# A new order of steps in a fused FFT and mixture kernel: fewer warming products, the first pair's maxima ahead of the next pair's folds, the third pair's product inside the last pair's

## The chip, the cores and the metric

The kernel runs on one core of one Trainium2 chip. The metric is device time in microseconds (us), the median of the runs of one kernel. The engines are PE (TensorE), DVE (VectorE), ACT (ScalarE), POOL (GpSimd) and SP, which issues every DMA of this kernel. Each engine works through its own queue in order.

## The reference, cut to what matters

```python
X = np.fft.fft(x, axis=1)            # x: 8 x 2496 x 256
X = np.fft.fft(X, axis=2).real       # then rows of 256: N = 19968 tokens
logits = x @ phi                     # 32 slots
d = exp(logits - logits.max(0)); d /= d.sum(0) + 1e-9     # over tokens
slot_input = d.T @ x                 # 8 experts x 4 slots
h = np.maximum(slot_input[e] @ w1[e], 0.0); slot_out[e] = h @ w2[e]
c = exp(logits - logits.max(1)); c /= c.sum(1) + 1e-9     # over slots
out = c @ slot_out                   # 19968 x 256
```

All data are float32. The input is 20 MB, the weights w1 and w2 are 17 MB, the output is 20 MB.

## The kernel before, in words

The eight sequences are handled as four pairs, p = 0 to 3. The Fourier transform is split (2496 = 39 x 64) and is never written out: its first steps give the logits, and the product of the softmax with the tokens is taken back to x through the transform. Each pair goes through the same chain of steps. A step has a letter, then the pair, then a part (t, half, or block), so `u20` is the product u of pair 2, first half. What each does, with its line and engine:

- f and F (L275, POOL, some DVE): fold a tile of x with its mirror tile xm, both loaded by SP (L208, L209); the mirror tiles share five buffers. F and A are second halves of tiles that are worked in halves.
- a and A (L304, DVE): transposes; z (L319, PE): first transform stage; t (L339, DVE): transposes out of PSUM; b and c (L353 or L381, L364 or L397, PE, evicted by ACT): the rest, which ends in the logits lt.
- n (L414, L417 or L421, DVE): maxima of the logits; i (L425 on PE, L427 and L429 on DVE) and j (L433 on PE, L435 on DVE): the maxima turned, spread and turned back to the tile nm; the end of j is the exponential d (L439, ACT, 11 of them per pair).
- e (L447 PE, L451 copies on DVE and ACT), d (L465 PE, L471 ACT): the transform back of the exponentials; G and H (L286 to L297, POOL and ACT): x folded once more; u (L487, PE): the product of both, into usb (L495) or, for the last pair, into acc (L578).
- k (L522, SP): loads of the weights, which go into buffers that x and other tiles leave; the last ones (steps k6 and k7) come behind the mirror tiles' last folds and the last u.
- m (L536 to L584): the four pairs are put together; m3 is the last pair's acc and its two products, m4 the result sT. l (L594 PE, L599 ACT, L601 DVE): w1, relu, transposes; V (L610): w2, eight steps for each half of the columns; R (L620) and r (L625, L626): the slots' result rh.
- s (L637 PE) and S (L655 ACT): logits turned to tokens on partitions; x, y, g, q (L664 to L684, DVE, POOL, ACT): softmax over slots; o and O (L702 PE, L711 copies on ACT and DVE, L714 DMA): the output.
- W (L328, PE): products of the identity with a table, whose result nobody reads; `W02` is two of them.

The order is written by hand: the table ORDER (lines 54 to 65) lists all steps, and the loop below runs them in that order and chains each instruction to the one before it on its own engine.

```python
        for what in ORDER:
            in_order(parts[what[0]], int(what[1]), int(what[2]))
```

So each engine's queue is the table read for that engine alone. Which buffer of a shared group a new tile gets, and so which earlier step its load waits for, is decided when the program is built, and follows from the order too.

Of the kernel before, what the change touches and what calls it, by code (L numbers as in the profile page):

```python
# [51 lines left out]
OB = (7, 2, 3, 0, 1, 4, 5)  # L52

ORDER = (
# [10 lines left out]
).split()  # L65


# [741 lines left out]
```

## Time and profile before

| what | value |
|---|---|
| median of 3 runs | 174.49 us (174.38 to 176.16) |
| the profiled execution's own time | 174.65 us |
| its span in the trace | 172.9 us |
| PE busy | 137.5 us (80%) |
| DVE busy | 111.4 us (64%) |
| POOL busy | 92.6 us (54%) |
| ACT busy | 84.7 us (49%) |
| DMA, mean over the span | 346 GB/s, 59.75 MB |

The kernel has stages with different limits, so the shares of the whole span say little. The rows below are read by stage: the loading of x up to about 58 us, a stretch in which PE and POOL work without a pause up to about 97 us, the experts up to about 119 us, and the output from there to the end. Times are from the span's start.

### The profile page before, as it was taken

To read this page: it belongs to the slowest core of one execution; us is meant where nothing else is said; L and a number is where in the kernel's file an instruction comes from. 1 tells how busy PE (TensorE), PEld (TensorE's weight loads), DVE (VectorE), ACT (ScalarE), POOL (GpSimd) and SP (SyncE) were. 2 spreads that over 40 slices of the span, in tenths; PEclk is the share of its full clock that TensorE was granted. 3 is DMA by queue.
4 is the path that set the end of the run, shared out by engine and by line. 5 is a ranking of instruction groups with operands and counts; after the bars stand their busy time and mean duration, and the time that the engine had idled before them with its cause. 6 is when DMAs were issued, how large, how long until landed. Compare 5 with 4: busy or idle time off the path is not lost.

```text
span 172.9 us, 5272 instructions
## 1 busy us (share of the span) xinstructions
PE 137.5 (80%) x2224; PEld 90.0 (52%) x2224; DVE 111.4 (64%) x213; ACT 84.7 (49%) x198; POOL 92.6 (54%) x64
## 2 busy tenths in 40 slices
PE   0798768599999999999969989999999697780000
PEld 0645645496754775578449573495655545340000
DVE  0396978798872899467055753975798987890000
ACT  2110113084332589368858715423789989670000
POOL 0004208998999999999999523550323654300000
PEclk9999999999999999999999999999999999996555
DMA  4999999999999970039999799902999999999993
GB/s 109 375 403 410 422 415 422 419 411 426 418 417 424 414 291 0 6 115 429 428 415 424 228 430 395 422 14 103 360 324 420 423 428 421 424 423 428 428 427 132
DMA packets 13559, 59.75 MB, mean 346 GB/s; under 512 B 1632, under 2 KB 2016, under 8 KB 10720
## 3 DMA queue, kind: packets, MB, share of 16 engines
q1 hardware_dynamic: 13536, 59.42, 85.2%
q8 instruction: 17, 0.28, 0.6%
q14 instruction: 6, 0.05, 0.1%
HBM read 38.96 MB, written 20.45 MB: 344 GB/s over the span
## 4 chain that ended last, share of the span: by engine, by line
PE 37%; DMA 22%; POOL 19%; ACT 5%; DVE 4%; issue 2%; SPq 0%; DVEq 0%; POOLq 0%; ACTq 0%
DMA xm<-xh 20%; PE ps L702 11%; POOL x L291 7%; POOL x L297 5%; PE ps L610 4%; PE ps L594 4%; ACT o L711 3%; PE ps L328 3%; PE ps L487 3%; PE ps L637 2%; PE ps L447 2%; POOL x L287 2%; POOL x L286 2%; DMA cs<-c 2%; POOL x L275 2%
## 5 line engine op out<-in xcount | busy, mean ns | idle before, releaser
L275 POOL TENSOR_TENSOR x<-x,xm 128x640 f32<-128x640 f32 (+1 forms) x11 | 23.8, 2167 | 23.7 <-DMA xm<-xh 23.5
L702 PE MATMUL ps<-ct,rh 32*128 32x512 f32 (+1 forms) x192 | 28.0, 545 | 3.9 <-ACT o L711 2.2
L711 ACT COPY o<-ps 128x512 f32<-128x512 f32 (+1 forms) x50 | 25.5, 623 | 5.4 <-PE ps L702 5.4
L319 PE MATMUL ps<-xT,wz 32*64 32x160 f32 (+1 forms) x768 | 22.3, 347 | 0.5 <-DVE xT L304 0.4
L702 PEld LDWEIGHTS ps<-ct,rh 32*128 32x128 f32 x192 | 14.7, 183 | 13.9 <-ACT o L711 9.0
L304 DVE STREAM_TRANSPOSE xT<-x 128x640 f32<-128x640 f32 (+1 forms) x18 | 18.8, 1055 | 3.0 <-POOL x L275 2.7
L439 ACT ACTIVATE d<-lt,nm 120x128 f32<-120x128 f32 x44 | 13.3, 388 | 13.8 <-DVE zt L335 7.0
L678 POOL TENSOR_TENSOR c<-c,cm 128x512 f32<-128x512 f32 (+1 forms) x8 | 10.1, 1264 | 16.8 <-DVE cm L677 10.0
L711 DVE COPY o<-ps 128x512 f32<-128x512 f32 (+1 forms) x29 | 17.9, 659 | 0.8 <-DMA out<-o 0.6
L665 POOL TENSOR_TENSOR c<-c,cm 128x512 f32<-128x512 f32 (+1 forms) x8 | 10.1, 1264 | 14.7 <-DVE cm L664 14.7
L319 PEld LDWEIGHTS ps<-xT,wz 32*64 32x64 f32 x768 | 14.2, 131 | 7.1 <-issue 2.9
L451 DVE COPY e<-ps 64x240 f32<-64x240 f32 x32 | 12.9, 405 | 3.5 <-PE ps L447 3.1
L339 DVE STREAM_TRANSPOSE zt<-ps 128x160 f32<-128x160 f32 (+1 forms) x24 | 11.7, 616 | 5.3 <-PE ps L319 5.3
L447 PE MATMUL ps<-cs,d 120*128 120x120 f32 x88 | 12.0, 291 | 2.6 <-ACT d L439 2.6
L487 PE MATMUL ps<-x,ds 128*32 128x129 f32 (+2 forms) x320 | 12.7, 302 | 0.4 <-POOL x L297 0.4
L447 PEld LDWEIGHTS ps<-cs,d 120*128 120x128 f32 x88 | 11.1, 190 | 3.6 <-ACT d L439 3.6
L291 POOL TENSOR_TENSOR x<-x 128x635 f32<-128x635 f32 x8 | 12.2, 1552 | 0.0
L297 POOL TENSOR_TENSOR x<-x 128x635 f32<-128x635 f32 x8 | 12.0, 1536 | 0.0
L275 POOL TENSOR_TENSOR xm<-x,xm 128x1280 f32<-128x1280 f32 x4 | 11.6, 2909 | 0.7 <-DMA xm<-xh 0.7
L487 PEld LDWEIGHTS ps<-x,ds 128*32 128x32 f32 x320 | 8.8, 110 | 3.5 <-issue 1.3
L275 DVE TENSOR_TENSOR x<-x,xm 128x640 f32<-128x640 f32 (+1 forms) x7 | 6.3, 907 | 5.3 <-DMA xm<-xh 5.3
L465 PE MATMUL ps<-e,cs 128*32 128x320 f32 x128 | 9.5, 435 | 0.2 <-ACT e L451 0.2
(105 smaller groups left out, 211.9 us busy)
## 6 DMA issues: line engine op xcount, KB each, us to landing
out<-o SPq DMA_DIRECT2D x13, 1024.0 KB, 11.1
w<-wh SPq DMA_DIRECT2D x9, 1280.0 KB, 10.8
x<-xh SPq DMA_DIRECT2D x12, 640.0 KB, 11.2
xm<-xh SPq DMA_DIRECT2D x12, 640.0 KB, 11.2
w<-wh SPq DMA_DIRECT2D x6, 640.0 KB, 11.6
out<-o SPq DMA_DIRECT2D x4, 896.0 KB, 10.5
out<-o SPq DMA_DIRECT2D x12, 256.0 KB, 3.4
x<-xh SPq DMA_DIRECT2D x8, 320.0 KB, 5.9
```

Of the source, the lines that this page charges most:

```text
L275: e.tensor_tensor(out[p, t][:, w], eo[p, t][:, w], xm[p, t][:, w], op=ALU.add)
L291: gp.tensor_tensor(lo, lo, hi, op=ALU.add)
L297: gp.tensor_tensor(hi, lo, hi, op=ALU.add)
L304: v.transpose(xT[p, ah][:, XW * h : XW * h + XW][:, w], (xm if p == LAST else eo)[p, t][:, w])
L319: pe.matmul(zb[p, h0][i][m, : 160 * n], wz[r, j % 4, j // 4], xv[r], start=j == 0, stop=j == 7, tile_position=(32 * i, 64 * ah),)
L339: v.transpose(o[:, :, NQ * i : NQ * i + NQ], zb[p, h0][i][:, : 160 * n].rearrange("p (h q s) -> p h q s", h=n, s=32),)
L439: sc.activation(d[:, g], lt[p][:, g0 + g], AF.Exp, bias=nm[:, g0 + g : g0 + g + 1], scale=1.0)
L447: pe.matmul(ps[:, 120 * g : 120 * g + 120], dd[p, b][:, g], C("ec"), start=True, stop=True)
L451: (v.tensor_copy if ECOPY[p][b] == "v" else sc.copy)(esb[p][64 * r : 64 * r + 64, :, h, GS * g0 : GS * (g0 + n)].rearrange("p c (g s) q -> ...
L487: pe.matmul(o, dsb[p][:, k, h, ah, q, :], xu[:, :, 128 * q : 128 * q + 128] if p == 0 else xu[:, D * q + c0 : D * q + c0 + w], start=cc == ...
L702: pe.matmul(po[:, j * w : j * w + w], rh[dc][rows], t[rows, r0 * NSLOT : r0 * NSLOT + w], start=True, stop=True, tile_position=(32 * g, 0),)
L711: (v.tensor_copy if evict[g] == "v" else sc.copy)(ot[:, o : o + w * len(dcs)], po[:, : w * len(dcs)])
```

## The change

Only the table ORDER changes. The diff shows its first line and the one with the third pair's product:

```diff
-    "w00 f00 a00 F00 W02 A00 f01 a01 z00 F01 A01 W01 z01 f02 a02 F02 f03 t00 A02 b00 a03 z02 F03 A03 z03 c00 f10 f11 "
+    "w00 f00 a00 F00 W01 A00 f01 a01 z00 F01 A01 z01 f02 a02 F02 f03 t00 A02 b00 a03 z02 F03 A03 z03 c00 t01 f10 f11 "
...
-    "G23 k30 u10 z33 k20 t30 u11 e20 e22 G30 H20 e21 b30 d20 H22 k40 k10 H21 T20 c30 c31 H23 G32 G33 n30 s00 u20 i30 "
-    "S00 k50 s01 j30 S01 e30 u21 e31 e32 s10 m00 k60 m10 s02 d30 S02 S10 T30 m20 u30 x00 k70 u31 m30 s12 x01 m40 S12 "
+    "k30 u10 z33 k20 t30 u11 e20 e22 G30 H20 e21 b30 d20 H22 k40 k10 H21 T20 c30 c31 H23 G32 G33 n30 s00 s01 i30 S00 "
+    "k50 j30 S01 u20 e30 u21 e31 e32 s10 m00 k60 m10 s02 d30 S02 S10 T30 m20 u30 x00 k70 u31 s12 m30 x01 m40 S12 l00 "
```

In words: `W02` becomes `W01`, and the `W01` ahead of z01 goes (three products become one). `t01` stands ahead of `f10`. `n01 i00 j00` stand ahead of or between `a11`, `A11` and `z10 z11`, and `t10` stands behind `a13`. `u20` moves from ahead of `i30` to behind `j30`, and `s01` from behind `i30` to ahead of it. `s12` stands ahead of `m30`, `l00` ahead of `y00 y01`, `O14` behind `O20`; `y11` and `y21` change places with `s20` and `o12`.

On PE, from the turned logits of pair 0 (tile lt) to the last pair's transform back (tile d_0), the queue of before reads as follows; x_0 with ds are the third pair's u20, mx and mex the last pair's maxima (i30, j30).

```order
L637 MATMUL ps<-cs_65,lt_319 128x120 x4
L487 MATMUL ps<-x_0_334,ds_1111 32x129 x2
L487 MATMUL ps<-x_0_334,ds_1111 32x128 x2
...
L425 MATMUL ps<-cs_65,mx_1169 11x120
L637 MATMUL ps<-cs_65,lt_319 128x120 x4
L433 MATMUL ps<-cs_65,mex_1200 120x11
L447 MATMUL ps<-cs_68,d_0_1214 128x120 x4
```

The same place in the changed kernel:

```order
L637 MATMUL ps<-cs_65,lt_317 128x120 x8
L425 MATMUL ps<-cs_65,mx_1167 11x120
L433 MATMUL ps<-cs_65,mex_1182 120x11
L487 MATMUL ps<-x_0_332,ds_1109 32x129 x2
L487 MATMUL ps<-x_0_332,ds_1109 32x128 x2
...
L447 MATMUL ps<-cs_68,d_0_1192 128x120 x4
```

The twenty matmuls of u20 and the second turn of the logits no longer stand between the maxima n30 and i30: both turns come first, then i30 and j30, then u20.

On DVE, from the first pair's second turn (zt) to the copies of its e (tile e), in the kernel before; x_0 and x_1 with L275 and L304 are the next pair's fold and transposes:

```order
L275 TENSOR_TENSOR x_0_106<-x_0_106,xm_0_107 128x1280
L339 STREAM_TRANSPOSE zt_220<-ps 128x5x32 x4
L304 STREAM_TRANSPOSE xT_0_370<-x_0_106 128x1280
L414 TENSOR_REDUCE mxh<-lt_319 120x11
L304 STREAM_TRANSPOSE xT_1_402<-x_1_110 128x640 x2
L414 TENSOR_REDUCE mxh<-lt_319 120x11
...
L304 STREAM_TRANSPOSE xT_0_370<-x_0_106 128x1280
L435 COPY nm_478<-ps 120x11
L335 MEMSET zt_494 128x2x24
L339 STREAM_TRANSPOSE zt_494<-ps 128x5x32 x4
L304 STREAM_TRANSPOSE xT_1_402<-x_1_110 128x640 x2
L451 COPY e_502<-ps 64x4x4x15 x8
```

And in the changed kernel:

```order
L339 STREAM_TRANSPOSE zt_218<-ps 128x5x32 x4
L275 TENSOR_TENSOR x_0_106<-x_0_106,xm_0_107 128x1280
...
L414 TENSOR_REDUCE mxh<-lt_317 120x11 x2
...
L435 COPY nm_411<-ps 120x11
L304 STREAM_TRANSPOSE xT_0_368<-x_0_106 128x1280
L304 STREAM_TRANSPOSE xT_1_403<-x_1_110 128x640
L335 MEMSET zt_493 128x2x24
L339 STREAM_TRANSPOSE zt_493<-ps 128x5x32 x4
L304 STREAM_TRANSPOSE xT_1_403<-x_1_110 128x640
L451 COPY e_500<-ps 64x4x4x15 x8
```

The turn zt comes ahead of the fold, both maxima ahead of the transposes of x_1, nm ahead of a12 (xT_0), and of the two half transposes a13 and A13 one stands on each side of the second pair's turn.

On SP, the loads of the third and fourth pair's mirror tiles, with the semaphores that each waits for (DMAHW0 to 7 are earlier loads, DVE and Pool the fold that frees the buffer), before:

```order
L209 DMA xm2_1_340<-xh 128x1280 [waits DMAHW2_49,DMAHW0_49,Pool_49]
L208 DMA x2_0_334<-xh 128x1280 [waits DMAHW1_49]
L209 DMA xm2_2_344<-xh 128x1280 [waits DVE_49]
L208 DMA x2_1_339<-xh 128x1280 [waits DMAHW3_49]
L209 DMA xm2_3_348<-xh 128x1280 [waits DMAHW4_49,DVE_49]
```

And in the changed kernel:

```order
L209 DMA xm2_1_338<-xh 128x1280 [waits DMAHW0_49,DVE_49]
L208 DMA x2_0_332<-xh 128x1280 [waits DMAHW1_49]
L209 DMA xm2_2_342<-xh 128x1280 [waits DMAHW2_49,Pool_49]
L208 DMA x2_1_337<-xh 128x1280 [waits DMAHW3_49]
L209 DMA xm2_3_346<-xh 128x1280 [waits DMAHW4_49,Pool_49]
```

The buffers go round in another order. The semaphores' values, which the rows don't print, say which fold each waits for: xm2_1 now waits for F03 instead of f12; xm2_2 for f12, xm2_3 for F13, xm3_0 to xm3_3 for f20 to f23, where before xm2_3 waited for f10 on DVE and xm3_0 to xm3_3 for F13, f20, f21 and f22. The buffer that f10 frees goes to a weight tile now.

## Rows read from the trace of the kernel before

**Rows 1.** The page's head, and its lines of 40 equal slices of 4.32 us: mean share of the DMA engines (tenths) and what they moved.
```profile
span 172.9 us, 5272 instructions
...
DMA  4999999999999970039999799902999999999993
GB/s 109 375 403 410 422 415 422 419 411 426 418 417 424 414 291 0 6 115 429 428 415 424 228 430 395 422 14 103 360 324 420 423 428 421 424 423 428 428 427 132
```

**Rows 2.** The output's DMAs: all 29 issues on SP in the timeline (start, time from the first to the last), and, in the list of DMAs, the one that is issued at 135.08 us (size and us to landing).
```profile
118.95 37.86 SPq L714 DMA_DIRECT2D out<-o  x29
...
out<-o SPq DMA_DIRECT2D x1, 1024.0 KB, 11.1
```

**Rows 3.** The chain of waits that ended last, between 88 and 99 us: start, length, engine and tile, line, instructions.
```profile
88.05 0.84 PE ps L487 x18
...
90.29 0.41 ACT d L439
...
90.74 1.36 PE ps L447 x8
...
93.33 1.77 PE ps L447 x14
...
96.46 2.37 PE ps L465 x31
```

**Rows 4.** The timeline around it (start, length, engine, line, operation, count; in brackets the idle time before and what ended it), and the e of the pair before at 58.16.
```profile
58.16 2.71 PE L447 MATMUL ps<-cs,d 120*128 120x120 f32 x22
...
84.97 6.01 POOL L297 TENSOR_TENSOR x<-x 128x635 f32<-128x635 f32 x4
...
86.29 1.74 DVE L421 TENSOR_REDUCE mx<-lt 120x4 f32<-120x512 f32 x3 [3.46 <-ACT lt L404]
...
88.83 0.27 PE L425 MATMUL ps<-cs,mx 120*11 120x120 f32 x1
...
90.29 3.33 ACT L439 ACTIVATE d<-lt,nm 120x128 f32<-120x128 f32 x11 [2.09 <-DVE nm L435]
...
92.03 1.30 PE L487 MATMUL ps<-x,ds 128*32 128x129 f32 x40
```

**Rows 5.** The chain of waits around m30, and from the timeline of DVE the copy `at` that m40 reads.
```profile
101.59 0.48 DVE acc L578 x2
...
102.93 0.46 PE ps L637 x3
103.39 0.27 PE ps L573 x2
...
102.97 0.22 DVE L584 COPY at<-ps 128x64 f32<-128x64 f32 x1 [0.91 <-PE ps L583]
```

**Rows 6.** The experts' second product V in the chain of waits, the load of the last large piece of weights in SP's timeline, and that load in the list of DMAs (the only issue between 100.4 and 101 us; the last number is us to landing).
```profile
112.03 3.93 PE ps L610 x144
...
100.49 0.33 SPq L522 DMA_DIRECT2D w<-wh  x1
...
w<-wh SPq DMA_DIRECT2D x1, 1280.0 KB, 13.4
```

**Rows 7.** DVE's timeline between the first transposes of l and the last transposes q01 of pair 0.
```profile
107.09 0.71 DVE L601 STREAM_TRANSPOSE hT<-hs 128x512 f32<-128x512 f32 x1 [2.47 <-ACT hs L599]
...
114.13 0.96 DVE L684 STREAM_TRANSPOSE ct<-c 128x768 f32<-128x768 f32 x1
```

**Rows 8.** The timeline between 32 and 41 us: transposes a12, the turn t10 and the copies of e0 on DVE, three folds on POOL (f13, F13, f20), z12 with z13 and then d00 on PE.
```profile
32.51 1.51 DVE L304 STREAM_TRANSPOSE xT<-x 128x1280 f32<-128x1280 f32 x1 [0.54 <-POOL x L275]
...
32.71 5.97 POOL L275 TENSOR_TENSOR x<-x,xm 128x640 f32<-128x640 f32 x3 [0.23 <-DMA xm<-xh]
...
34.06 1.46 DVE L339 STREAM_TRANSPOSE zt<-ps 128x160 f32<-128x160 f32 x4
...
36.82 3.32 DVE L451 COPY e<-ps 64x240 f32<-64x240 f32 x8
...
37.97 2.45 PE L319 MATMUL ps<-xT,wz 32*64 32x160 f32 x128
...
40.35 2.38 PE L465 MATMUL ps<-e,cs 128*32 128x320 f32 x32
```

**Rows 9.** The timeline at the third pair's z20: the weight loads of its first matmuls, and what ended the idle time before them.
```profile
50.07 0.20 PEld L319 LDWEIGHTS ps<-xT,wz 32*64 32x64 f32 x6 [0.23 <-DVE xT L304]
```

**Rows 10.** The start: the view of line 328 (ns min/median/max, first and last start), DVE's transpose a01 and z00 in the timeline, and the windows view of PE between 12 and 13 us (length, PE busy and its instructions, granted clock, DMA share, GB/s).
```profile
L328 PE MATMUL ps<-cs,cs x6: 592/1061/1061, 9.5 to 14.9; 128*128 128x512 f32 x6
...
11.08 0.84 DVE L304 STREAM_TRANSPOSE xT<-x 128x640 f32<-128x640 f32 x1
...
13.03 1.42 PE L319 MATMUL ps<-xT,wz 32*64 32x160 f32 x64
...
12.00:13.00 1.00, 1.00 (x2) 1.00 1.04 415
```

**Rows 11.** The chain's last wait for a mirror tile (xm3_3, issued at 45.37), and the folds f22 and f23 on POOL.
```profile
45.37 12.30 DMA xm<-xh
...
42.39 5.97 POOL L275 TENSOR_TENSOR x<-x,xm 128x1280 f32<-128x1280 f32 x2 [0.20 <-DMA xm<-xh]
```

14 rows, old and new, of the table ORDER are left out of this document.

## The prediction

> **What bounds the kernel now.** I read the page's slices first. Of the 172.9 us, the DMA engines are full from the second slice to about 58 us, idle to about 78, full again to about 112, and full from about 125 us to the end [rows 1]. So the start is paced by the loading of x, and the end by the output: the first output goes out at 118.95 us, the 20 MB then leave at 420 to 428 GB/s for most of the time [rows 1, 2], and an output tile that is issued at 135.08 lands 11.1 us later [rows 2]: a queue stands before the DMA engines that covers small delays of single tiles. The end therefore moves with the start of the output, and that hangs on the chain before it.
>
> The chain of waits shows that chain between 88 and 99 us: on PE 18 matmul rows of u20 after a wait for POOL, then i30, j30, the first exponential on ACT, e30, u21, e31 with e32, and d30 at 96.46 [rows 3]. The timeline adds what the chain leaves out: the maxima n30 on DVE run from 86.29 for 1.74 us, so they end at 88.03, but i30 starts at 88.83, because u20 stands ahead of it in PE's queue [rows 4].
>
> **The change part by part.**
>
> *u20 and s01 behind and ahead of i30.* With only s00 and s01 ahead (done long before 88), i30 starts at 88.05 instead of 88.83: 0.78 us earlier. From i30 to the first exponential nothing is touched (88.83 to 90.29, 1.46 us [rows 4]), so the exponentials start at 89.51, one each 0.303 us (3.33 / 11), the fourth done at 90.72. PE has finished j30 by 89.20 and does u20 while ACT works: 40 rows, 1.30 us as u21 takes [rows 4], to 90.50. That is later than e30 could have begun (89.96 by the same distance as before), so a part of the 0.78 is paid back here. But e30 then finds three of its four exponentials done, and runs at the pace of an e that waits for nothing, 2.71 / 22 = 0.123 us a row [rows 4]: 8 rows, 0.98 us, to 91.48, where it took 1.36 [rows 3]. Then u21 to 92.78; its last fold is through by 84.97 + 6.01 = 90.98 [rows 4]. Then e31 and e32, 1.77 us [rows 3], to 94.55. Before, they ended at 95.10. The gain on the path is 0.55 us. The copies of e32 and d30 follow at the same distance, since the eviction by ACT is what d30 waits for in both. Of the 0.78 us, 0.23 goes into u20 standing ahead of e30.
>
> *s12 ahead of m30.* PE waits for acc on DVE (101.59, 0.48 us) with nothing to do, then runs m30, and s12 fills the next gap from 102.93, to 103.39, when m40 starts; m40's input `at` is done at 102.97 + 0.22 = 103.19 [rows 5]. With s12 in the first gap (0.46 us in 0.48), m40 starts at about 103.23: 0.16 us.
>
> *l00 ahead of y00 and y01.* On ACT the first relu no longer stands behind two exponentials. PE is not waiting for it, so the path gains nothing. But DVE waits 2.47 us for that relu before it can start at 107.09, and then works to 114.13 + 0.96 = 115.09 [rows 7] on what stands ahead of the copy R00 of V's result. V ends at 112.03 + 128 x 3.93 / 144 = 115.52 [rows 6]. So DVE has 0.43 us to spare: without this edit the gain would stop there. With it DVE starts earlier by the path's gain and a part of the 2.47 us more, and the cap is off.
>
> *The weights.* The last large piece is issued at 100.49 and lands 13.4 us later, at 113.89 [rows 6], through full DMA engines [rows 1]; its issue is held by loads ahead of it that wait for POOL, which the change leaves alone. V needs it after 6.5 of its 8 steps. With V's start earlier by 0.65 this is at 111.38 + 6.5 / 8 x 3.49 = 114.22: 0.33 us after the landing. So the path can give about 1.0 us before it runs into the weights.
>
> *The early edits: t01, n01, i00, j00, t10.* They bring the first pair's exponentials forward by more than 2 us, as nm no longer stands behind a12, which waits for POOL until 32.51 [rows 8]. But the first use of them that counts is the copies of e0 on DVE, and these stand behind a12, a13, t10 and A13, whose folds come as x comes. Before: t10, a13 and A13 run from 34.06 to 36.82, without a wait, 2.76 us. Now a13 stands first and must wait for f13 on POOL, the first of three folds from 32.71 (two halves and a whole in 5.97 us, so a half is about 1.5 us): to 34.25. The copies start at about 34.27 + 2.76 = 37.03 instead of 36.82, and end at 40.35 instead of 40.14. d00 on PE began at 40.35, after z13 [rows 8]; now z13 is done earlier and d00 waits for the copies, to about 40.40. The loss is 0.05 us, and PE runs on from there without a gap to z20 at 50.07, whose wait is for DVE's transpose of folded x [rows 9]. So earlier work cannot gain here, and later work loses at once: bounds 0 and 0.25 us (the whole shift of the copies), I take 0.06. What queues behind the waiting a13 on DVE is t10, A13 and those copies, and for them waits d00.
>
> *The two products fewer.* W02 and W01 hold PE, so z00 starts at 13.03, while its last input a01 is there at 11.08 + 0.84 = 11.92 [rows 10]. Without them z00 begins 1.1 us and z01 about 2 us earlier. All of it is swallowed before a12, by the cover just named: 0.
>
> *The mirror tiles' buffers.* The order also turns the buffers: four of the fourth pair's loads wait for a fold one later than before. The last, xm3_3, was issued at 45.37 and landed at 57.67 [rows 11]; now it must wait for f23, which ends at 42.39 + 5.97 = 48.36 [rows 11]: 3.0 us later. Ahead of it stand then five loads of 0.655 MB, at 420 GB/s [rows 1] 1.56 us each, 7.8 us of work. So the DMA engines don't run dry and it lands when it did: 0. With the cover gone it would cost up to 3.0 us, since the folds, POOL's long stretch and the last weights all start from it.
>
> *The rest* (O14 behind O20, y11, y21) lies in the output, where 11 us of queued output cover it [rows 2]: 0.
>
> **Sum.** -0.55 - 0.16 + 0.06 = -0.65 us on the start of the output and, since the output's own work moves with it, on the end. Against the profiled execution, 174.65 us (1.75 us of it around the span of 172.9), that is 174.0. That execution lies 0.16 above the median of the runs, 174.49, so the forecast is 173.85 us.
>
> **The rivals.**
>
> 1. *The gain is swallowed, no change.* The early loss is larger than I take it (POOL's half fold f13 comes later when DMA is late; each 0.1 us goes straight through PE to z20 and on to n30), or the last weights land later. It takes 0.6 us in all. For it speaks that z20 has no slack and the weights 0.33 us; against it that the copies of e0 can shift only by 0.25. Time: 174.3 to 174.7.
>
> 2. *Slower: the loading of x runs dry.* With one buffer fewer in the round, the mirror loads go out behind POOL's folds. If the queue ahead of xm3_3 were empty at 48.36, up to 3.0 us would be lost at the fourth pair's folds, and all of it reaches the output through POOL and the last weights (1.0 us of room less): 174.5 + 2 to 3, about 177. It decides from the point at which f23 ends 7.8 us later than it did. Against it: in the kernel before xm2_1 stood behind f12 in just this way, and the slices around it, from 26 to 39 us, moved 411 to 422 GB/s [rows 1].
>
> 3. *Slower: PE stays at half clock.* The granted clock stands at full (1.00) at 12 to 13 us, yet the product rows of line 328 took 1.061 us at the start and 0.592 later [rows 10]: the first ones are paid at what looks like half speed. With two products fewer z00 and z01 may be worked at 1.2 GHz; that costs them 1.4 us each at most, and is hidden ahead of a12 too. Only if it lasted to z13 would it show: z10 with z11 and z12 with z13, 2.45 us each pair [rows 8], and e0, 2.7 us as the e at 58.16 [rows 4], would take twice their time, 7.6 us more, of which some 2 us are spare before a12: about 179.5 us.
> The Trainium skill ("TensorE: Matmul & The Clock Gate", "What's actually happening") has the clock throttled by default and released by activity, and so speaks against taking warming products away; by it the products' removal may cost what rival 3 says. No run here shows a half clock past 14 us.
>
> 4. *More: about 1 us.* If e30 begins between the rows of u20, or the weights land earlier, the path gives the whole 0.78 + 0.16 and a little: 173.4.
>
> **How the numbers follow.** My forecast (173.5 to 174.2) has 0.62, rival 1 0.2, rival 4 0.08, rivals 2 and 3 together 0.06, something else in the output's order 0.04, half of it to each side. The range 173.2 to 174.6 holds the forecast, rival 4 and most of rival 1. A measurement of this kernel tells about 1% (1.74 us) from no change. The forecast, rival 1 and rival 4 lie within it: faster by over 1% 0.02, within 0.90, slower 0.08.
>
> **What would show it.** In the changed kernel's trace: i30 right behind n30's end (88.05), u20 between j30 and e30, d30 near 95.9, m40 0.04 us behind `at`, V's end near 114.9 and the first output near 118.3. xm3_3 issued near 48.4 and landed near 57.7 would prove the buffers harmless, DMA slices below 400 GB/s before 58 us would prove rival 2, and z rows twice as long past 14 us rival 3. I am wrong if PE's stretch from 40 us to 88 starts later by more than 0.3 us, or if V waits for weights.

## The result, and the profile after

The changed kernel takes 176.88 us (median of 20), the kernel before beside it 174.86 us: ratio 1.0114, 95% interval 1.0085 to 1.0143. It is slower by about 2 us, outside the predicted range and on the other side of the forecast. (Executions over 1.5% longer than the fastest of their kernel are left out of every ratio.) The profiled execution of the changed kernel took 176.79 us.

The page's head and slices of the changed kernel; the second line is the granted clock in tenths, the third answers to the GB/s of [rows 1].

```profile
span 175.0 us, 5263 instructions
...
PEclk9999999699999999999999999999999969659755
...
GB/s 101 371 412 410 426 411 421 418 423 414 420 416 429 327 303 0 6 32 381 418 421 420 328 412 401 412 34 89 362 264 414 428 429 421 431 421 425 431 429 142
```

The same clock line of the kernel before:

```profile
PEclk9999999999999999999999999999999999996555
```

The loading of x is as full as it was (410 to 429 GB/s in slices 3 to 13), so rival 2 is out at first sight. The eighth slice of the clock (30.6 to 35 us) has a 6. That is the place to look at first. PE's timeline there (its last row is cut off by the end of the window), from the maxima of pair 0 (i00 on line 425, j00 on line 433) over z10 with z11, e0, z12 with z13 and d00 to z20; it answers to [rows 8, 9].

```profile
29.59 0.26 PE L425 MATMUL ps<-cs,mx 120*11 120x120 f32 x1 [1.80 <-DVE mx L417]
30.70 0.24 PE L433 MATMUL ps<-cs,mex 11*120 11x11 f32 x1 [0.85 <-DVE mex L429]
30.87 3.77 PE L319 MATMUL ps<-xT,wz 32*64 32x160 f32 x101
35.40 0.79 PE L319 MATMUL ps<-xT,wz 32*64 32x160 f32 x27 [0.76 <-issue]
36.11 2.71 PE L447 MATMUL ps<-cs,d 120*128 120x120 f32 x22
38.76 1.62 PE L319 MATMUL ps<-xT,wz 32*64 32x160 f32 x78
41.41 1.24 PE L319 MATMUL ps<-xT,wz 32*64 32x160 f32 x50 [1.03 <-issue]
42.58 2.38 PE L465 MATMUL ps<-e,cs 128*32 128x320 f32 x32
...
52.30 1.93 PE L319 MATMUL ps<-xT,wz 32*64 32x320 f32 x38
```

and on DVE, in the same execution, the transposes a12 and the copies of e0:

```profile
32.65 1.51 DVE L304 STREAM_TRANSPOSE xT<-x 128x1280 f32<-128x1280 f32 x1 [1.20 <-POOL x L275]
...
38.30 3.32 DVE L451 COPY e<-ps 64x240 f32<-64x240 f32 x8
```

d00 starts at 42.58 instead of 40.35 [rows 8], z20 at 52.30 instead of 50.07 [rows 9]: both 2.23 us late. So the prediction's own sign of being wrong has come, PE's stretch from 40 us on later by more than 0.3 us. Three things stand in the way that were not there: PE waits for i00 and j00 with nothing else to do, the 101 rows of z behind them are slow, and twice PE stops for "issue", which is time in which it waits for nothing that the profile shows. The windows of the same stretch (length, PE busy and its instructions, granted clock, DMA share, GB/s) explain the slow rows.

```profile
28.00:29.00 1.00, 0.00 (x0) 1.00 1.01 420
...
30.00:31.00 1.00, 0.30 (x5) 0.88 1.02 425
31.00:32.00 1.00, 1.00 (x24) 0.50 1.07 445
...
33.00:34.00 1.00, 1.00 (x48) 0.50 1.00 406
34.00:35.00 1.00, 0.63 (x29) 0.91 1.01 410
```

PE did almost nothing from 28 to 31 us; then the granted clock is 0.50, which is 1.2 GHz, until about 34 us.

The late part went by the prediction's list. DVE's maxima n30 and PE's rows behind them, and the first output on SP, from timelines of the changed kernel, against [rows 2, 4, 5]:

```profile
88.52 1.74 DVE L421 TENSOR_REDUCE mx<-lt 120x4 f32<-120x512 f32 x3 [3.46 <-ACT lt L404]
90.32 0.27 PE L425 MATMUL ps<-cs,mx 120*11 120x120 f32 x1 [0.84 <-DVE mx L421]
91.25 0.22 PE L433 MATMUL ps<-cs,mex 11*120 11x11 f32 x1 [0.66 <-DVE mex L429]
91.41 1.30 PE L487 MATMUL ps<-x,ds 128*32 128x129 f32 x40
92.63 1.15 PE L447 MATMUL ps<-cs,d 120*128 120x120 f32 x8
...
98.14 2.37 PE L465 MATMUL ps<-e,cs 128*32 128x320 f32 x32 [0.19 <-ACT e L451]
104.93 0.41 PE L573 MATMUL ps<-at,cs 128*128 128x32 f32 x2 [0.32 <-DVE at L584]
...
120.63 41.02 SPq L714 DMA_DIRECT2D out<-o  x29
```

i30 stands right behind n30 (90.26), u20 between j30 and e30, and n30's end to d30 takes 7.88 us, where it took 96.46 - 88.03 = 8.43. The first output still goes out 1.68 us late (118.95 before): 2.23 lost early, 0.55 given back.

### The profile page after: what moved, and what is told of

It is laid out like the page before. It is cut to its first block, busy times and chain, and to the rows that moved or that the text cites. A ratio compares the mean times of both kernels' runs of the same rounds, so it can differ in the third digit from the quotient of the medians.

```text
span 175.0 us, 5263 instructions
## 1 busy us (share of the span) xinstructions
PE 138.9 (79%) x2220; PEld 93.7 (54%) x2220; DVE 112.2 (64%) x213; ACT 84.6 (48%) x198; POOL 92.6 (53%) x64
## 4 chain that ended last, share of the span: by engine, by line
PE 65%; DVE 9%; DMA 8%; ACT 4%; SPq 3%; issue 3%; DVEq 0%
PE ps L702 14%; PE ps L319 11%; PE ps L487 7%; PE ps L447 6%; PE ps L465 5%; PE ps L381 4%; PE ps L610 4%; PE ps L594 4%; PE ps L397 4%; DMA xm<-xh 4%; DMA x<-xh 4%; DVE o L711 2%; DVE cm L675 1%; PE ps L637 1%; SPq L208 1%
## 5 line engine op out<-in xcount | busy, mean ns | idle before, releaser
L275 POOL TENSOR_TENSOR x<-x,xm 128x640 f32<-128x640 f32 (+1 forms) x11 | 23.7, 2165 | 23.4 <-DMA xm<-xh 22.9
L702 PE MATMUL ps<-ct,rh 32*128 32x512 f32 (+1 forms) x192 | 30.1, 636 | 5.4 <-ACT c L655 3.0
L319 PE MATMUL ps<-xT,wz 32*64 32x160 f32 (+1 forms) x768 | 25.4, 379 | 3.2 <-issue 1.8
L702 PEld LDWEIGHTS ps<-ct,rh 32*128 32x128 f32 x192 | 17.7, 215 | 14.6 <-ACT o L711 7.3
L319 PEld LDWEIGHTS ps<-xT,wz 32*64 32x64 f32 x768 | 16.7, 149 | 9.9 <-issue 4.6
L304 DVE STREAM_TRANSPOSE xT<-x 128x640 f32<-128x640 f32 (+1 forms) x18 | 18.9, 1059 | 2.7 <-POOL x L275 2.5
L711 DVE COPY o<-ps 128x512 f32<-128x512 f32 (+1 forms) x29 | 18.4, 665 | 2.5 <-PE ps L702 2.5
L275 POOL TENSOR_TENSOR xm<-x,xm 128x1280 f32<-128x1280 f32 x4 | 11.6, 2910 | 1.0 <-DMA xm<-xh 0.6
L447 PE MATMUL ps<-cs,d 120*128 120x120 f32 x88 | 11.1, 280 | 0.0
L447 PEld LDWEIGHTS ps<-cs,d 120*128 120x128 f32 x88 | 10.2, 191 | 1.2 <-ACT d L439 1.0
L451 ACT COPY e<-ps 64x180 f32<-64x180 f32 x16 | 5.0, 311 | 8.8 <-PE ps L447 8.7
```

Of the source, the lines that this page charges most:

```text
L275: e.tensor_tensor(out[p, t][:, w], eo[p, t][:, w], xm[p, t][:, w], op=ALU.add)
L304: v.transpose(xT[p, ah][:, XW * h : XW * h + XW][:, w], (xm if p == LAST else eo)[p, t][:, w])
L319: pe.matmul(zb[p, h0][i][m, : 160 * n], wz[r, j % 4, j // 4], xv[r], start=j == 0, stop=j == 7, tile_position=(32 * i, 64 * ah),)
L447: pe.matmul(ps[:, 120 * g : 120 * g + 120], dd[p, b][:, g], C("ec"), start=True, stop=True)
L451: (v.tensor_copy if ECOPY[p][b] == "v" else sc.copy)(esb[p][64 * r : 64 * r + 64, :, h, GS * g0 : GS * (g0 + n)].rearrange("p c (g s) q -> ...
L702: pe.matmul(po[:, j * w : j * w + w], rh[dc][rows], t[rows, r0 * NSLOT : r0 * NSLOT + w], start=True, stop=True, tile_position=(32 * g, 0),)
```

## The experiments

"The piece at z10" is the part of ORDER with n01, i00, j00 and t10. "The late pieces" are u20 behind j30 with s01 ahead, s12 ahead of m30, l00 ahead of y00 and y01. `W02` or `W12` is two unread products of line 328; with the 1 in the middle they go to another PSUM bank (line 326 then has `bank(7 if i else WB)`, in e3, e6, e10, e11 and e13). A theory's letter, and what it foresees, stands in the expectation of the run.

The traces left two explanations of the 2.23 us at z20, theory A (PE idles ahead of i00 and j00, and then works at half clock) and theory B (PE stops for its next instructions). Their rivals were that another early edit made the loss, or the two products fewer.

**Which piece.**

```diff
e1, against the changed kernel:
-n01 a11 i00 A11 j00 z10 z11 a12 a13 t10 A13 e00
+a11 A11 n01 z10 i00 z11 a12 j00 t10 a13 A13 e00
```

> The changed kernel with one piece of the table put back as before: a11 A11 n01 z10 i00 z11 a12 j00 t10 a13 A13 (n01, i00, j00 and t10 where they were); all else as changed. Theory M (the 2.2 us were lost because i00 and j00 stand ahead of z10 and z11 on PE): z20 starts within 0.3 us of 50.07, against 52.30 after the change, and the time is 0.4 to 0.9 us under the kernel before, since the late gains of 0.56 and 0.14 us stay. Rival theory R (one of the other early edits, the two products fewer or t01, or the mirror tiles' buffers, made the loss): z20 stays at 52 or later and the time about 1.5 to 2 us over before.

Measured: 175.16 us, ratio to before 1.0003 (0.9976 to 1.0030). The loss goes with the piece at z10, as theory M has it and rival R has not. M's figures were not met: in the profiled execution z20 is at 51.33, not within 0.3 us of 50.07, since e0 took 4.48 us, the clock at 0.50 from about 35.5 to 38.9 us, and the gain that should have been left isn't there.

```diff
e2, against before:
-a11 A11 n01 z10 i00 z11 a12 j00 t10 a13 A13 e00
+n01 a11 i00 A11 j00 z10 z11 a12 a13 t10 A13 e00
```

> The kernel before with that one piece alone changed: n01 i00 j00 ahead of or between a11, A11 and z10 z11, t10 behind a13. Theory M: z20 starts near 52.3, PE shows pauses between 34 and 42 us that nothing in the trace releases, the granted clock falls to 0.50 between 31 and 34 us, and the time is 2.0 to 2.8 us over before (2.2 early, and no late gain). Rival theory R (another early edit): z20 near 50.1 and the time within 0.4 us of before. A third possibility, that it takes the piece and the two products fewer together: z20 between 50.4 and 51.5.

Measured: 175.77 us, 1.0044 (1.0017 to 1.0070): 0.8 us over before, less than in the changed kernel and less than the 2.0 to 2.8 us of theory M. The clock fell (0.50 from about 31.4 to 38.2 us), but no pause for "issue" appeared. The profiled execution (177.05 us) was longer than most; another one of the same kernel:

> A second look at the kernel before with the piece around z10 alone. Its profiled execution took 177.05 us, with 0.50 from 31.3 to 38 us and z20 at 52.85, while the median was 175.8. By theory A an execution near 175.8 has a shorter stretch at 0.50 and z20 at 51.2 to 51.8; if the stretch is as long and z20 as late, the difference lies elsewhere.

Measured: 176.30 us. Its timeline (z10 with z11, e0, z12 with z13, d00, z20):

```profile
32.25 4.63 PE L319 MATMUL ps<-xT,wz 32*64 32x160 f32 x128
36.81 2.72 PE L447 MATMUL ps<-cs,d 120*128 120x120 f32 x22
39.45 2.45 PE L319 MATMUL ps<-xT,wz 32*64 32x160 f32 x128
42.43 2.37 PE L465 MATMUL ps<-e,cs 128*32 128x320 f32 x32 [0.53 <-DVE e L451]
...
52.15 2.20 PE L319 MATMUL ps<-xT,wz 32*64 32x320 f32 x46
```

With half clock (0.50 from about 33.4 to 36.8 us) and without any pause z20 is 2.08 us late, more than the 1.1 to 1.7 us that theory A had said for a shorter stretch.

```diff
e5, against the changed kernel:
-W01 A00 ... A01 z01
+W02 A00 ... A01 W01 z01
```

> The changed kernel with the two unread products put back where they stood before (two ahead of z00, one ahead of z01); n01, i00, j00 and t10 stay as changed. It asks whether the two products fewer have a part in the loss. Theory S (PE's idle stretch before i00 and j00 makes the loss, whatever came before): z00 and z01 are about 1.5 us later, i00 still waits about 1.8 us for DVE and j00 0.85, the granted clock still falls to 0.50 just behind, z20 lies between 51.5 and 53, and the time stays 1.2 to 2.2 us over before. Theory P (the products keep the clock up): no row of 0.50 between 27 and 44 us, z20 near 50.3, the time within 0.4 us of before.

Measured: 177.38 us, 1.0133 (1.0104 to 1.0163); the clock is at 0.50 from about 30.0 to 36.8 us, around i00 again, and there are pauses of 0.46 and 0.69 us. Theory S: putting the two products back doesn't take the loss away. (It is slightly over S's 1.2 to 2.2 us.)

```diff
e9, against before:
-c00 f10 f11 t01 F11
+c00 t01 f10 f11 F11
-a11 A11 n01 z10 i00 z11 a12 j00 t10 a13 A13 e00
+n01 a11 i00 A11 j00 z10 z11 a12 a13 t10 A13 e00
```

> The kernel before with t01 ahead of f10 and with the piece around z10 (n01 i00 j00 ahead, t10 behind a13), and nothing else; the products and all late pieces as before. It asks why the piece around z10 costs 0.4% by itself and 1.1% in the changed kernel. Theory T (t01 early brings PE's pause before i00 forward by about 1 us, so that z10 starts with too few instructions loaded): z10 starts near 31.4, pauses that nothing releases behind it, and the time 1.8 to 2.6 us over before. Rival theory L (the late pieces or the output's pieces add to it): z10 near 32.4, no such pauses, and the time 0.5 to 1.1 us over before, as with the piece alone.

Measured: 176.79 us, 1.0114 (1.0091 to 1.0137), the whole loss of the changed kernel, with pauses of 0.94 and 1.05 us and z20 at 52.73. Theory T holds: t01 early and the piece at z10 together make it, and the piece alone doesn't (e2).

**Half clock or instructions.** Unread products fill the time in which PE waits.

```diff
e3, against the changed kernel:
-c01 n01 a11 i00 A11 j00 z10
+c01 W13 n01 a11 i00 W11 A11 j00 z10
e6, e10 and e11 (one kernel), against the changed kernel:
-c01 n01 a11 i00 A11 j00 z10
+c01 W12 n01 a11 i00 A11 j00 z10
```

> The changed kernel with four unread products of line 328 (the identity with a table, 0.59 us each at full clock) put where PE waits for DVE: three ahead of i00, one between i00 and j00, into a PSUM bank that z10 takes next. So PE has work from 27.8 to about 31 us. Theory A (the 2.2 us come from z10 and z11 being worked at half clock): the granted clock stays at 1.00 between 30 and 36 us, z10 with z11 take 2.6 us for their 128 rows rather than 4.6, z20 starts near 50.3 to 50.8, and the time falls about 1.5 to 2 us under the changed kernel. Theory B (PE runs out of instructions since z10 and z11 follow each other without a wait, and the next block's load is asked for only there): the clock is full, but the pauses that nothing releases stay between 33 and 42 us and become longer, z20 stays near 52, and the time stays within 0.5 us of the changed kernel.

Measured: 175.02 us, 1.0017 (0.9986 to 1.0048). No row below 1.00 between 26 and 46 us, z20 at 51.00, one pause of 0.32 us. i00 itself started 1.36 us later than in the changed kernel, behind the products, so not all could come back.

> The changed kernel with two unread products (1.83 us by the six rows of the run with more of them: 2.74 us for three) ahead of i00 only, in the stretch from 27.8 to 29.6 us in which PE waits for DVE. Theory A (half clock on z10 and z11 is most of the loss): i00 starts near 29.7, z10 and z11 take 2.9 us, the clock stays at 1.00 to 44 us, z20 starts at 50.1 to 50.5, and the time is 0.2 to 0.7 us under before (the late gains show). Theory B (pauses that nothing releases are most of it): pauses of 1 us or more between 33 and 42 us, z20 at 51 or later, the time not below before.

Measured: 176.79 us, 1.0087 (1.0054 to 1.0120), though the profiled execution took 175.04 us. Its timeline (z10 with z11, on DVE a12 and the copies of e0, d00, z20):

```profile
31.24 3.00 PE L319 MATMUL ps<-xT,wz 32*64 32x160 f32 x128
...
33.00 1.51 DVE L304 STREAM_TRANSPOSE xT<-x 128x1280 f32<-128x1280 f32 x1 [1.16 <-POOL x L275]
...
37.56 3.31 DVE L451 COPY e<-ps 64x240 f32<-64x240 f32 x8
...
41.02 2.38 PE L465 MATMUL ps<-e,cs 128*32 128x320 f32 x32 [0.88 <-DVE e L451]
...
50.73 2.99 PE L319 MATMUL ps<-xT,wz 32*64 32x320 f32 x64
```

Full clock, no pause, and z20 within 0.3 us of what theory A had said. It is 0.66 us later than before, but 0.49 of that is x: a12, which waits for POOL's fold, starts at 33.00 instead of 32.51 [rows 8]. The other executions were longer, most of them at the same mean clock (0.93 to 0.94). Two more executions of it were profiled:

> A second look at the changed kernel with two unread products ahead of i00. Its profiled execution took 175.04 us with z20 at 50.73, but the median was 176.8, at the same mean granted clock. If this execution takes over 176.3 us, its trace shows what the longer ones have: by theory B pauses of 1 to 2 us in all that nothing releases between 33 and 42 us, at full clock; by theory A a stretch at 0.50; by a third, neither, and the loss behind 90 us. If it takes about 175, z20 is again near 50.7.

> A third look at the same kernel, for the same question and with the same numbers.

Measured: 178.08 and 178.94 us. e10 has a pause of 2.35 us at full clock ahead of z11's last rows, and behind it the clock at 0.50 from about 37.3 to 40.7 us, in which e0 took 4.34 us. The timeline of e11, from the second half of b01 on:

```profile
25.68 0.81 PE L353 MATMUL ps<-cs,zt 128*64 128x64 f32 x21 [0.34 <-issue]
...
31.33 2.46 PE L319 MATMUL ps<-xT,wz 32*64 32x160 f32 x97
36.13 0.80 PE L319 MATMUL ps<-xT,wz 32*64 32x160 f32 x31 [2.35 <-issue]
36.87 2.71 PE L447 MATMUL ps<-cs,d 120*128 120x120 f32 x22
39.51 1.59 PE L319 MATMUL ps<-xT,wz 32*64 32x160 f32 x74
42.15 1.31 PE L319 MATMUL ps<-xT,wz 32*64 32x160 f32 x54 [1.05 <-issue]
...
53.24 1.12 PE L319 MATMUL ps<-xT,wz 32*64 32x320 f32 x14
```

and two of the windows of e11:

```profile
33.00:34.00 1.00, 0.79 (x43) 1.00 1.07 436
34.00:35.00 1.00, 0.00 (x0) 1.00 0.98 399
```

The clock is 1.00 from 28 to 46 us, and still z20 is 3.17 us later than before, behind pauses of 2.35 + 1.05 us. (The rest of this execution's 178.94 us lies elsewhere: i30 to d30 took 1.6 us longer, at a lower clock.) Theory B is right for e11; e10 has a pause and a half clock behind it.

The rows tell what the pauses are. Between the pause in b01 and the next stand 21 rows of b01, 4 of c01, 4 of the products, i00, j00 and 97 of z: 128 matmuls, with a weight load each 256 instructions. Then 31 of z, 22 of e0 and 74 of z, 127 in all, to the next. The DMA view has a queue of its own for them. Before, between 24 and 33 us (packets, MB, share of 16 engines):

```profile
q8 instruction: 1, 0.02, 0.7%
```

In the changed kernel no such line stands in that stretch; its packet comes in the window from 33 to 34 us:

```profile
q8 instruction: 1, 0.02, 6.0%
```

Narrow windows give each packet's start. In the 16 pauses for "issue" of the traces, those in b01 with them, PE resumes 2.22 to 2.44 us after one (changed kernel: 33.18 and 35.40, 39.11 and 41.41). While x is loaded, one packet follows another by 5.76 us at the least.

| kernel (run) | piece at z10 as changed | PE stops in b01 | load behind the one near 23 us | pauses, 31 to 43 us | z20 |
|---|---|---|---|---|---|
| before | no | no | 29.39 | 0 | 50.07 |
| late pieces (e4) | no | no | 29.63 | 0 | 50.06 |
| before with products (e7) | no | no | 29.16 | 0 | 49.95 |
| late pieces, products (e8) | no | no | 29.82 | 0 | 50.84 |
| piece undone (e1) | no | 0.34 | 29.51 | 0 | 51.33 |
| piece undone, products (e14) | no | 0.33 | 29.21 | 0 | 50.05 |
| piece alone (e2, e12) | yes | no | 29.46, 29.48 | 0 | 52.85, 52.15 |
| products (e6) | yes | no | 28.94 | 0 | 50.73 |
| more products (e3) | yes | 0.73 | 29.59 | 0.32 | 51.00 |
| changed | yes | 0.09 | 33.18 | 1.79 | 52.30 |
| products back (e5) | yes | 0.40 | 33.60 | 1.15 | 53.09 |
| t01 and piece (e9) | yes | 0.28 | 33.27 | 1.99 | 52.73 |
| the same kernel as e6 (e10, e11) | yes | 0.59, 0.34 | 34.16, 33.69 | 2.35, 3.40 | 53.65, 53.24 |

(0.09 and 0.28 are what b01's 44 rows took over 1.50 us. e8 shows how far z20 moves by itself: full clock, no pause, the early steps of e7, and 0.77 us later than before, a12 at 33.00 as in e6.) Where PE comes to the border in b01 before the load of 23 us is there, and the piece at z10 is as changed, the next load is 4 us late in five of six traces; in the traces of the piece without that stop (e2, e12, e6) it never is. In the traces with t01 early PE begins b01 at 24.29 to 24.91 us (24.42 in the changed kernel), without it at 25.37 to 26.21 (25.70 before). The last test delays it there:

```diff
e13, against the changed kernel:
-a10 n00 b01 c01
+a10 n00 W11 b01 c01
```

> The changed kernel with one unread product (0.9 us) ahead of b01, so that PE reaches row 19 of b01 near 26.0 us, after the landing of the instruction load that starts near 23.3 (it lands 2.3 us later, near 25.6). The waits at i00 and j00 stay. Theory R (PE reaching that point before the landing is what makes the next load late): no pause inside b01, the next load near 29.4, no pauses that nothing releases between 33 and 43 us, but still a stretch at 0.50 behind i00; the time 0.2 to 1.0 us over before, as with the piece around z10 alone. Rival theory W (PE's wait at i00 is what makes it late): the next load at 33 or later, pauses of 1 us or more, and the time 1.8 us or more over before.

Measured: 176.10 us, 1.0063 (1.0029 to 1.0097). The profiled execution was one of the longer ones (177.89 us), c00 already 2.0 us later than in the changed kernel, so that b01 was held back by 3.06 us and not by the product alone. Only its pattern is read: no stop in b01, loads at 24.36 and 30.31, no pause up to z20, and 0.50 from about 34.7 to 38.1 us. This is theory R's pattern, the half clock of the piece without the pauses. The time, 1.1 us over before by the ratio, is just above R's 0.2 to 1.0 and under the 1.8 of theory W.

**The late pieces, and versions that could beat both.**

```diff
e4, against before:
-s00 u20 i30 S00 k50 s01 j30 S01 e30 ... m30 s12 x01 m40 S12 y00 y01 l00
+s00 s01 i30 S00 k50 j30 S01 u20 e30 ... s12 m30 x01 m40 S12 l00 y00 y01
e7, against before:
-a12 j00 t10
+a12 j00 W02 t10
e8: e4 and e7 together. e14: e1, and the W02 of e7 behind its j00.
```

> The kernel before with the late pieces alone changed: u20 behind j30 with s01 ahead of i30, s12 ahead of m30, l00 ahead of y00 and y01. Everything up to 86 us as before, z20 at 50.07. By the working of the prediction the first output goes out 0.70 us earlier (0.56 + 0.14 as the changed kernel's trace has them), near 118.25, and the time is 0.5 to 0.8 us under before. Rival: the output's own work doesn't follow, since other waits stand in it (the changed kernel lost 0.4 us more there than the 1.68 us by which its first output was late): the time is then within 0.2 us of before though the first output goes out 0.70 us earlier.

Measured: 175.22 us, 0.9995 (0.9965 to 1.0024). In the profiled execution, 174.11 us, z20 is at 50.06, d30 at 95.91 and the first output at 118.40, 0.55 us ahead of before, and the time 0.54 us less than before's own profiled execution.

> The kernel before with two unread products more, behind j00 and ahead of e00, where PE waits 1.81 us for the first exponential. If the half clock behind such a wait is what makes some executions of the kernel before longer than others (its mean granted clock goes from 0.93 to 0.95 between executions), the products take it away: e0 at full clock, the median 0.2 to 0.5 us under before. If e0 was mostly at full clock anyway, nothing: within 0.2 us. If e00 is held up by the products (1.83 us for a gap of 1.81): up to 0.1 us over.

Measured: 174.64 us, 0.9983 (0.9961 to 1.0006). In the profiled executions of both kernels e0 is at full clock anyway (3.41 us, before 3.42), so the traces show nothing that the products could take away.

> The same, and the late pieces too (u20 behind j30 with s01 ahead of i30, s12 ahead of m30, l00 ahead of y00 and y01). Against the run with the products alone it tells what the late pieces are worth in the time: first output 0.55 to 0.7 us earlier, and by the prediction's working the time 0.5 to 0.7 us less; by the rival (the output's stage gives the gain back, through its own waits and clock) within 0.2 us of it. It is also the version that could beat both kernels: 174.0 to 174.4 if both parts hold.

Measured: 174.63 us, 0.9987 (0.9959 to 1.0014). Against e7, which lacks the late pieces alone, that is 0.01 us: the 0.5 to 0.7 us of the prediction's working don't show in the time, and the expectation's rival (within 0.2 us) fits.

> The changed kernel with the piece around z10 as before and two unread products behind j00, ahead of e00. e0 was at half clock in the profiled execution without them (4.48 us where it takes 3.4) and z20 at 51.33. If that was what the change without the piece still lost, z20 is at 50.0 to 50.4, and the time 0.4 to 0.8 us under before; if the early edits that are left or the output's moves lose it elsewhere, within 0.2 us of before.

Measured: 174.42 us, 0.9986 (0.9960 to 1.0012). Its timeline (z20, d30, first output):

```profile
50.05 2.98 PE L319 MATMUL ps<-xT,wz 32*64 32x320 f32 x64
...
95.89 2.37 PE L465 MATMUL ps<-e,cs 128*32 128x320 f32 x32 [0.20 <-ACT e L451]
...
118.38 41.09 SPq L714 DMA_DIRECT2D out<-o  x29
```

So with two products ahead of e0 z20 is back where e1 had lost it, in one execution of each. On the path the traces give 0.55 us for u20's move; that the time follows isn't shown: each of these four intervals holds both no change and a gain of 0.55 us (0.31%), and e8 beside e7 shows none. A version that measurably beats the kernel before wasn't found.

## Why the prediction was wrong

**The failed step is the early edits, taken at +0.06 with bounds 0 and 0.25.** It followed the queue of DVE alone, from f13 over a13 and t10 to the copies of e0, and took PE's z rows as if they would run at the old pace whenever their input was there. In the changed kernel i00 and j00 stand ahead of z10 on PE and wait 1.80 + 0.85 us for DVE. The sum had nothing for PE's work behind that wait, which met two prices: half clock (e12: z20 2.08 us late, no pause) and instructions that came late (e11: 3.17 us, full clock). Each alone made z20 over 2 us late in an execution. By the ratios the piece alone, with no pause in its two traces, lost 0.8 us, and e6's kernel, with full clock up to z11 in its three traces, 1.5 us.

DVE's own part was right. In e6, with neither price, the copies of e0 start 37.56 - 33.00 = 4.56 us behind a12; foreseen were 37.03 - 32.51 = 4.52. Without the later x, e6's z20 is 0.17 us late, inside the bounds. In the changed kernel both prices are there: 128 rows of z took from 30.87 to 36.19, 5.3 us, of it 0.76 pause, against 3.0 at full clock (e6). t10 on DVE then waits for z11, and the copies start 5.65 us behind a12, at 38.30 instead of the 37.03 foreseen: 1.09 us more than in e6. The second pause, 1.03 us, delays z13, and d00 starts 4.28 us behind the copies' start, in e6 3.46: 0.82 more. With the 0.17, and 0.14 of later x (a12 at 32.65), that is the 2.23 us within 0.01. In e12 the half clock by itself is 1.6 of the 2.08 us: z10 with z11 take 4.63 instead of 3.00, and 0.27 is later x (a12 at 32.78). How the 1.09 divides between half clock and the first pause isn't separated.

**Rival 3** had the half clock past 14 us, but hung it on the products. Putting them back didn't help (e5), and filling PE's idle time from 28 to 31 us kept the clock at 1.00 there (e3, e6). The prediction saw in that edit only exponentials that come forward by more than 2 us, and no wait for PE. Its sentence that no run showed a half clock past 14 us was a misreading: the clock line of the kernel before has it from about 156.5 us on, where PE has nothing left to do. Its hidden part came and stayed hidden: z00 with z01 took 3.80 us (before 1.42 + 1.37), and b00 still began at 16.78 us instead of 18.41. And its price of 7.6 us was too high, since the clock was back by the time e0 ran (at about 34 us, in e12 37). The Trainium skill ("TensorE: Matmul & The Clock Gate", "What's actually happening") has the clock fall when PE idles and says that the moment of a change varies between executions. The traces agree: 0.50 behind the idle stretch in every trace of the piece at z10 without products in it, from 30.8 us in the changed kernel, from about 33.4 in e12.

**u20 and s01 (-0.55)** was right on the path: d30 came 0.55 us sooner in e4 and 0.57 in e14. But it only pays while PE is on time. In the kernel before u20 waits 0.43 us for POOL, and i30 starts 38.76 us behind z20:

```profile
88.05 0.84 PE L487 MATMUL ps<-x,ds 128*32 128x128 f32 x18 [0.43 <-POOL x L297]
```

In e9, with the old order and PE late, the same rows (n30 on DVE, u20, i30, d30):

```profile
88.96 1.74 DVE L421 TENSOR_REDUCE mx<-lt 120x4 f32<-120x512 f32 x3 [3.46 <-ACT lt L404]
...
89.43 1.30 PE L487 MATMUL ps<-x,ds 128*32 128x129 f32 x40
90.75 0.27 PE L425 MATMUL ps<-cs,mx 120*11 120x120 f32 x1
...
98.38 2.37 PE L465 MATMUL ps<-e,cs 128*32 128x320 f32 x32 [0.20 <-ACT e L451]
```

u20 runs in one go under the maxima, i30 comes right behind them, 38.02 us behind z20, and from n30's end to d30 it is 7.68 us, 0.20 less than in the changed kernel. So a delay x of z20 (above 0.74) arrives at d30 as x - 0.74 in the old order and as x - 0.55 in the new: e2 2.78 and 2.04, e12 2.08 and 1.34, changed 2.23 and 1.68, e1 1.26 and 0.72. For a PE that is late the new order is even 0.2 us the slower one. The gain was the removal of a wait that a late PE doesn't meet. That is why e9, without the late pieces, is as slow as the changed kernel.

**s12 ahead of m30 (-0.16)** was 0. m40 starts 6.79 us behind d30 in both kernels (104.93 - 98.14; before 103.25 - 96.46). The prediction took 103.39 from the chain [rows 5]; the chain lets a step begin where the one before ends, and matmuls overlap. The timeline has m40 at 103.25, 0.06 us behind `at`: there was nothing to gain.

**The rest held.** The two products: 0 (e14 has z20 at 50.05 without them). The mirror tiles: xm3_3 was issued at 48.08 and landed 9.5 us later, at 57.58 (48.4 and 57.7 foreseen). l00 ahead of y00 and y01: 0, the first output stands 15.70 us behind m40 in both kernels. V ran its 144 rows without a wait for weights (113.53, 4.11 us). The output's moves: from the first output to the end of the span 54.4 us after and 53.95 before [rows 1, 2], 53.8 to 54.4 in the kernels with O14 in either place, so 0 within that spread. (The 0.4 us that the changed kernel's span has over before beyond the 1.68 lies there.)

**Open.** What asks for the next instruction load isn't shown, nor why e3 escapes the late one, nor why e0 met half clock in e1 and not in the kernel before, behind the same wait of 1.81 us. e13 shows only that in one execution that reached the border in b01 later the next load was on time.

## What to carry to other kernels

When a step is moved ahead of work that PE used to have in hand, price the wait that PE gets, and then PE's own work behind it: look for a lower granted clock and for pauses marked "issue" in the first rows after it. A gain that consists in removing a wait has to be checked against the other terms of the sum: if one of them makes the waiting engine late, the wait and the gain are gone. Start times come from the timeline; a chain's segments begin where their predecessor ends.

## What the runs showed of the hardware

PE can outrun its instructions. By the rows between pauses a load of 0.02 MB serves 256 instructions, and one follows the last by 5.76 us or more while the DMA engines are full of x; z10 with z11 use up as many in 3.0 us (e6). Then PE stands for up to 2.35 us, at full clock and waiting for nothing else that the profile shows (e11). The Trainium skill ("Runtime: NRT & Kernel Launch", "Instruction fetch mechanics") has the stream refilled in blocks of 256 instructions, which the rows bear out, and calls the crossing of a border mostly hidden; here it wasn't, with 1.79 us of pauses in the changed kernel and 3.40 in e11, and the measurement decides.

One kernel gave executions of 175.04 and 178.94 us (e6, e11). One such load came at 28.94 us in the first and at 33.69 in the second, and z20 at 50.73 and 53.24, which is 2.5 of the 3.9 us. The other 1.6 us, between i30 and d30, have the clock at 0.50 from about 92.7 to 96.1 us in e11.
